# A fused attention and gated feed-forward kernel: weights converted in two VectorE passes, 42 tiles through the DMA crossbar instead of 28, and a new written order

## The chip, the cores and the metric

The kernel runs on one core of one Trainium2 chip. The metric is device time in microseconds (us) of that core, the median of several runs. A core has five engines with a queue each: TensorE (PE in the profile, PEld for its weight loads), VectorE (DVE), ScalarE (ACT), GpSimd (POOL) and SyncE (SP), which here only issues DMAs. A DMA's data is moved by 16 shared DMA engines. PE writes its results into PSUM, a small memory that VectorE and ScalarE can read.

## The reference

Eight batches, eight heads, 576 tokens, 64 columns per head, all fp32. Attention keeps only the scores within `tau` of a row's maximum; its output (512 columns) goes through a feed-forward layer with a gate that is a convolution over three tokens:

```python
scores = scale * np.matmul(q, k.transpose(0, 1, 3, 2))
thresh = np.max(scores, axis=-1, keepdims=True) - tau
scores = np.where(scores >= thresh, scores, -1000000000.0)
attn = np.exp(scores - np.max(scores, axis=-1, keepdims=True))
attn = attn / (np.sum(attn, axis=-1, keepdims=True) + 1e-09)
x = np.matmul(attn, v)                      # heads side by side: 512 columns
h = np.maximum(x @ w_in, 0.0)               # 1024 columns
conv = sum(conv_w[k] * hp[:, k:k + S] for k in range(3))   # hp: h, padded by one token
out = (h / (1.0 + np.exp(-conv))) @ w_out
```

The weights `w_in`, `w_out` and `conv_w` come as float64, which the chip has no arithmetic for: the kernel puts each together from its two 32-bit words.

## The kernel before, in words

**Pairs, tiles, chunks.** Heads go in pairs, four pairs to a batch. The 576 query rows of a batch are four tiles of 128 and one of 64; a batch is done in two chunks, tiles 0 and 1 and then tiles 2, 3 and 4. A *unit* is one tile of one pair; there are 160, counted in order (units 0 to 19 are the first batch). Odd pairs take the tiles of a chunk in reverse.

**A unit** (`unit`, L552). PE makes the scores of both heads into two PSUM tiles `ps_s` (L573 for the first batch, in plain fp32, and for 64-row tiles; L580 for the rest, with q in two parts). For each head VectorE takes the row maximum (L588), ScalarE the exponential (L597), one of three engines the limit "maximum minus tau" (L594, L592), and VectorE masks the exponentials by it and sums them (L600). Small steps make the inverse of the sum (L617, L624) and a shift for rows whose sum is zero (L621), and GpSimd normalises `em` (L633). There are two `ps_s` buffers, so the scores of the next unit wait for the masks of this one.

**Turning `em`.** The product with V needs `em` turned. For most tiles PE does it with 128x128 transposes (L692), and ScalarE takes them out of PSUM into `eT` (L687). Twenty-eight tiles, one for each even pair of each chunk from the second batch on (`CROSS`, L54 and L646), go through the DMA crossbar instead (`cross`, L648): ScalarE and GpSimd split `em` into its 16-bit halves (`parts`, L326 and L328), SP writes them to DRAM (`rows`, L665) and issues two crossbar transfers into `eT` (L670). PE then multiplies with V (L747, L756); from the third chunk on it does so for two pairs at a time, once both are turned.

**Feed-forward.** `mm1` (L772) multiplies by `w_in` (L784), with values and weights each in a high and a low part; then come ReLU (L799), two taps (L806), tanh (L813), gate (L811) and a split of the result (L821, L333). GpSimd sets the padding columns of `hp` each time (L794, L796). `mm2` (L833) multiplies by `w_out` (L842) and writes the output.

**Weights** (`split`, L353). Sixteen pieces of 128x512 are loaded during the first batch. For each: ScalarE takes the absolute value of the upper word (L377), GpSimd clamps it (L380), VectorE shifts it (L383), puts the sign in (L386) and adds bits of the lower word (L389); ScalarE rounds this to the high part (L400), and PE or GpSimd makes the low part (L405, L406, L333). The convolution weights need a row of some fifteen small VectorE steps more (`ratios`, L452 to L456).

**What sets the order.** Every step is recorded with a cost, a due time and its dependences (`Plan.op`, L101). `Plan.run` (L120) walks through them with assumed latencies (`LATENCY`, `late`) and writes each engine's instructions down in the order in which that walk picks them; ready steps go by due time less a lead (`AHEAD`), and PE stays with one kind of matmul for a while (`KEEP`). What it writes is fixed: on the chip every engine takes its queue strictly in this order and waits where an input is missing. The program spreads the feed-forward work of a chunk between the units of the next.

Of the kernel before, what the change touches and what calls it, by code (L numbers as in the profile page):

```python
# [19 lines left out]
TINY = 2.0 ** -15  # L20
HUGE = 3.0e38
AHEAD = {'s': 6.25, 's4': 7.75, 't': 3.5, 'a': 3.5, 'prep': 4.25, 'w': 2.5, 'load': 7.75}

LATENCY = {"pe": 210.0, "act": 145.0, "dve": 110.0, "pool": 75.0, "ring": 950.0}

HOLD = {"pool": 165.0, "dve": 130.0}

NORM = (('pool',), ('pool',))

NEAR = 8  # L30
# [5 lines left out]
WRATE = (1.225, 1.745)  # L36
ALT = 11.76
# [216 lines left out]
def tile_tau_attention_gated_ffn(  # L254
# [59 lines left out]
    ntau = const("ntau", [P, 1], F32)  # L314
    op("dve", 70, lambda: nc.vector.tensor_scalar(ntau[:], tau_sb[:], -1.0, None, op0=ALU.mult), w=[(ntau, 0)], r=[(tau_sb, 0)], ahead=6.0)
# [20 lines left out]
    def put(n, fn, issue=460, rows=P, queue="sp", **kw):  # L336


        op(queue, issue, fn, ring=rows * (n * 0.225 + 4) * 0.0737, **kw)
# [13 lines left out]
    def split(src, n, name, high, low, hr, lr, queue="sp"):  # L353
# [4 lines left out]
        value = plan.buf(wk, "q2", 2, [P, 2, 2 * P], U32, f"{name}_f")  # L358
# [17 lines left out]
        def f0():  # L376
            nc.scalar.activation(v(), words(F32)[1], AF.Abs)  # L377

        def f1(e):
            engines[e].tensor_scalar(v(), v(), HUGE, TINY, op0=ALU.min, op1=ALU.max)  # L380

        def f2():
            nc.vector.tensor_scalar(v(U32), v(U32), 3, 0x3FFFFFF8, op0=ALU.logical_shift_left, op1=ALU.bitwise_and)  # L383

        def f3():
            nc.vector.scalar_tensor_tensor(v(U32), words()[1], 0xC0000000, v(U32), op0=ALU.bitwise_and, op1=ALU.bitwise_or)  # L386

        def f4():
            nc.vector.scalar_tensor_tensor(v(U32), words()[0], 29, v(U32), op0=ALU.logical_shift_right, op1=ALU.bitwise_or)  # L389
# [40 lines left out]
    def load_conv():  # L430
# [25 lines left out]
        op("dve", 1100, ratios, w=[(cw, 0), (cr, 0)], r=[(cwl, 0)])  # L456
# [49 lines left out]
    def halves(dst, src, of, ahead):  # L506

        x, view, parts = src
        for part, head in of:
# [5 lines left out]
                ), issue=560, rows=D,  # L515
# [17 lines left out]
    def prep_q(i, b, p, q1, q2):  # L533
# [5 lines left out]
        op("act", act(w), lambda: nc.scalar.activation(q1[:, 0], xq[:], AF.Copy), w=[(q1, (0, 0)), (q1, (0, 1))], r=[(xq, 0)], ahead=a)  # L539
        op(  # L540
            "pool", pool(w), lambda e: subtract(e, q2[:, 0], xq[:], q1[:, 0].bitcast(F32)),
            w=[(q2, (0, 0)), (q2, (0, 1))], r=[(xq, 0), (q1, (0, 0)), (q1, (0, 1))], ahead=a, other=[("dve", dve(w))], port=True
        )
        for q in (q1, q2):
            halves(q, (q, Later(lambda q=q: q[:, 0], w), ((0, 0), (0, 1))), [((1, 1), 1), ((1, 0), 1), ((0, 1), 0)], a)

    def load_v(i, b, p):
        vt = plan.buf(wk, "v", 2, [P, NBLK, D], F32, f"v_{i}")
# [3 lines left out]
    def unit(u, k, q1, q2, o, n):  # L552
# [7 lines left out]
        few = plan.buf(sm, "few", 4, [P, 10], F32, f"few_{u}")  # L560
        a = AHEAD["s" if 2 * n > P else "s4"]
        tiny = [("pool", 200)]
        for h, js in enumerate(heads):
            ps = plan.buf(ps_s, "ps_s", 2, [P, 2, 512], F32, f"ps_s_{u}_{h}")
            nm, th, total = (slice(at + h, at + h + 1) for at in (0, 2, 4))

            def mm(h=h, js=js, ps=ps):
                if q2 is None:
                    for r, j in enumerate(js):
                        for c in range(2):  # L570
# [3 lines left out]
                                ps[r * n:(r + 1) * n, c, :CH], lhsT=q1[on, j, o:o + n], rhs=k[on, at:at + CH],  # L574
# [3 lines left out]
                for c in range(2):  # L578
                    for i, q in enumerate((q1, q2)):
                        nc.tensor.matmul(  # L580
                            ps[:, c, :CH], lhsT=q[:, h, o:o + n], rhs=k[:, h, c * CH:(c + 1) * CH], start=(i == 0), stop=(i == 1)
                        )
# [7 lines left out]
            def limit(e, nm=nm, th=th):  # L590
                if e == "act":
                    nc.scalar.activation(few[:rows, th], few[:rows, nm], AF.Identity, scale=-1.0, bias=ntau[:rows])  # L592
                else:
                    engines[e].tensor_scalar(few[:rows, th], few[:rows, nm], -1.0, ntau[:rows], op0=ALU.mult, op1=ALU.add)  # L594
# [4 lines left out]
            def mask(ps=ps, th=th, view=view, total=total):  # L599
# [411 lines left out]
```

## Time and profile before

| | |
|---|---|
| three runs | 912.18, 912.48, 914.12 us; median 912.48 us |
| span of the profiled execution | 910.8 us |
| mean granted TensorE clock in it | 0.993 |
| DMA traffic | 137.02 MB, mean 150 GB/s |
| SP's DMA issues | 336 copies `q<-q`, 64 loads of v, 28 writes of `rows`, 56 crossbar transfers |

The profile shows one execution; its own time is known as the span, from the first to the last instruction. The median of the runs lies 1.7 us above the span, so what lies around the span is about that. Each row of a group has the line of the kernel, the engine, the operation, what it writes and reads, and how often; then its busy time in us, the mean of one in ns, and the idle time of the engine just before it. Matmuls overlap, so what one of them takes from PE is read from one start to the next, not from its own length.

### The profile page before, as it was taken

How to read it: one execution, taken by the hardware profiler on the slowest of the kernel's cores; microseconds unless marked ns; L12 is line 12 of the kernel's file. 1: busy time of each engine (PE TensorE's matmuls, PEld its weight loads, DVE VectorE, ACT ScalarE, POOL GpSimd, SP SyncE). 2: the span in 40 equal slices, each digit the busy share in tenths (PEclk: the TensorE clock that was granted, in tenths of full speed). 3: DMA queues.
4: the chain of work that ended last, by engine and by line, in shares of the span. 5: the costliest groups of instructions: out<-in, count | busy, mean ns of one | idle time of the engine just before them, and what ended most of it. 6: DMA issues, size and time to landing. Idle time of an engine off the chain costs nothing.

```text
span 910.8 us, 19147 instructions
## 1 busy us (share of the span) xinstructions
PE 874.6 (96%) x6056; PEld 708.6 (78%) x6056; DVE 751.2 (82%) x1871; ACT 673.8 (74%) x1459; POOL 603.5 (66%) x1027
## 2 busy tenths in 40 slices
PE   5978799999999999999999999999999999999998
PEld 3545577878878788888788797887888878887896
DVE  5988999988988689987889789996988779997542
ACT  4878687878777777777768687877867778776642
POOL 2656778875767677685767767776776758675322
PEclk9989899999999999999999999999999999999999
DMA  6555257667764667647665377557667276654000
GB/s 213 155 162 170 57 143 197 149 178 181 198 175 113 163 175 198 158 116 202 169 157 157 117 201 191 140 118 202 173 176 179 89 187 159 181 137 112 13 24 35
DMA packets 148260, 137.02 MB, mean 150 GB/s; under 512 B 85312, under 2 KB 116288, under 8 KB 148160
## 3 DMA queue, kind: packets, MB, share of 16 engines
q1 hardware_dynamic: 147296, 133.90, 55.3%
q10 hardware_dynamic: 864, 1.90, 0.6%
q8 instruction: 49, 0.80, 0.4%
q14 instruction: 51, 0.42, 0.2%
HBM read 58.88 MB, written 25.95 MB: 93 GB/s over the span
## 4 chain that ended last, share of the span: by engine, by line
PE 73%; ACT 8%; DVE 6%; POOL 5%; DMA 4%; issue 3%; SPq 2%; ACTq 0%; POOLq 0%; DVEq 0%
PE po L842 20%; PE ph L784 16%; PE pa L756 12%; PE ps_s L580 11%; PE ps_t L692 9%; PE ps_s L573 3%; ACT em L597 2%; POOL em L633 2%; DVE em L600 2%; ACT eT L687 2%; PE pa L747 2%; DVE few L588 2%; DMA q<-in_qd_dram 1%; SPq L513 1%; DMA q<-q 1%
## 5 line engine op out<-in xcount | busy, mean ns | idle before, releaser
L633 POOL TENSOR_SCALAR em<-em,few 128x576 f32<-128x576 f32 x287 | 262.8, 924 | 29.9 <-DVE few L624 22.1
L600 DVE SCALAR_TENSOR_TENSOR em<-ps_s,few,em 128x576 f32<-128x576 f32 x288 | 230.5, 812 | 25.4 <-ACT em L597 17.1
L588 DVE TENSOR_REDUCE few<-ps_s 128x1 f32<-128x576 f32 x288 | 211.5, 748 | 39.3 <-PE ps_s L573 22.0
L597 ACT ACTIVATE em<-ps_s,few 128x576 f32<-128x576 f32 x288 | 210.5, 741 | 35.8 <-DVE few L588 31.5
L784 PE MATMUL ph<-x,w1h 128*128 128x322 f32 (+1 forms) x1024 | 233.7, 304 | 0.6 <-ACT hp L799 0.5
L687 ACT ACTIVATE eT<-ps_t 128x512 f32<-128x512 f32 (+2 forms) x360 | 168.0, 487 | 24.5 <-PE ps_t L692 22.4
L784 PEld LDWEIGHTS ph<-x,w1h 128*128 128x128 f32 x1024 | 173.1, 189 | 4.7 <-issue 3.0
L692 PE MATMUL ps_t<-ident,em 128*128 128x128 f32 x1060 | 157.8, 280 | 6.5 <-POOL em L633 5.1
L580 PE MATMUL ps_s<-ks,q 128*128 128x288 f32 x896 | 156.8, 306 | 5.3 <-DMA q<-q 2.1
L784 PE MATMUL ph<-x,w1l 128*128 128x322 f32 (+1 forms) x512 | 151.3, 295 | 0.0
L692 PEld LDWEIGHTS ps_t<-ident,em 128*128 128x128 f32 x1060 | 126.5, 143 | 31.5 <-POOL em L633 14.9
L580 PEld LDWEIGHTS ps_s<-ks,q 128*128 128x128 f32 x896 | 129.2, 189 | 20.2 <-issue 8.2
L333 POOL TENSOR_TENSOR gl<-t,gh 128x255 fp32r<-128x255 f32 (+9 forms) x192 | 119.6, 637 | 28.5 <-ACT gh L821 27.5
L756 PE MATMUL pa<-eT,v 128*64 128x320 f32 (+1 forms) x1024 | 132.1, 410 | 0.0
L842 PE MATMUL po<-w2h,gh 128*128 128x512 f32 x288 | 117.9, 409 | 0.3 <-ACT hp L799 0.3
L756 PEld LDWEIGHTS pa<-eT,v 128*64 128x64 f32 x1024 | 70.4, 137 | 59.3 <-issue 15.8
L842 PE MATMUL po<-w2l,gh 128*128 128x512 f32 x288 | 113.3, 393 | 0.0
L842 PE MATMUL po<-w2h,gl 128*128 128x512 f32 x288 | 113.1, 393 | 0.1
L806 DVE SCALAR_TENSOR_TENSOR t<-hp,cr 128x321 f32<-128x321 f32 (+1 forms) x128 | 75.6, 594 | 28.0 <-ACT hp L799 28.0
L784 PEld LDWEIGHTS ph<-x,w1l 128*128 128x128 f32 x512 | 96.8, 189 | 0.2
L813 ACT ACTIVATE t<-t,cm 128x321 f32<-128x321 f32 (+1 forms) x128 | 68.0, 535 | 25.2 <-DVE t L806 12.2
L811 DVE SCALAR_TENSOR_TENSOR t<-t,hp 128x321 f32<-128x321 f32 (+1 forms) x128 | 73.1, 573 | 11.4 <-ACT t L813 9.8
(80 smaller groups left out, 1104.1 us busy)
## 6 DMA issues: line engine op xcount, KB each, us to landing
q<-q SPq DMA_DIRECT2D x336, 64.0 KB, 2.1
v<-in_vc_dram SPq DMA_DIRECT2D x64, 288.0 KB, 3.8
rows<-parts SPq DMA_DIRECT2D x28, 576.0 KB, 3.3
k<-in_kp_dram SPq DMA_DIRECT2D x35, 320.0 KB, 3.5
out_dram<-ot SPq DMA_DIRECT2D x36, 256.0 KB, 2.3
xk<-in_kt_dram SPq DMA_DIRECT2D x28, 288.0 KB, 3.4
ks<-xk SPq DMA_DIRECT2D x56, 144.0 KB, 3.3
xq<-in_qt_dram SPq DMA_DIRECT2D x56, 128.0 KB, 2.9
```

Source lines behind the costliest of these rows:

```text
L333: engines[e].tensor_tensor(dst, x, y, op=ALU.subtract)
L580: nc.tensor.matmul(ps[:, c, :CH], lhsT=q[:, h, o:o + n], rhs=k[:, h, c * CH:(c + 1) * CH], start=(i == 0), stop=(i == 1))
L588: nc.vector.tensor_reduce(few[:rows, nm], ps[:rows, :, :CH], op=ALU.max, axis=mybir.AxisListType.XY, negate=True)
L597: nc.scalar.activation(view(), ps[:rows, :, :CH], AF.Exp, bias=few[:rows, nm])
L600: nc.vector.scalar_tensor_tensor(view(), ps[:rows, :, :CH], few[:rows, th], view(), op0=ALU.is_ge, op1=ALU.mult, accum_out=few[:rows, total])
L633: engines[e].tensor_scalar(sl, sl, by, to, op0=ALU.mult, op1=ALU.add)
L687: "act", act(w, True), lambda dst=dst, src=src: nc.scalar.activation(dst(), src(pt), AF.Copy),
L692: nc.tensor.transpose(out=pt[:, at:at + P], in_=em[:, int(b * P):int(b * P) + P], identity=ident[:])
L756: nc.tensor.matmul(pa[j * D:(j + 1) * D, :w], lhsT=vt[:, blk, :], rhs=eT[:, :w // D, blk, :], start=False, stop=(r == 3))
L784: nc.tensor.matmul(ph[:, :an], lhsT=w1[w][:, cb, fs], rhs=xs[cb][:, h, :an], start=(cb == 0 and i == 0), stop=(cb == NCB - 1 and i == 2))
L806: nc.vector.scalar_tensor_tensor(t[:, :kn], hp[:, k:kn + k], cr[:, j, f:f + 1], y, op0=ALU.mult, op1=ALU.add)
L842: nc.tensor.matmul(po[:], lhsT=x[:, f, at:at + P], rhs=w[:, f, :], start=(f == 0 and i == 0), stop=(f == NFB - 1 and i == 2))
```

## The change

The lines of the changed kernel are given as it has them; they are up to 28 further down.

- **Crossbar.** `CROSS` now depends on chunk and pair. In a batch's first chunk even pairs cross one tile as before; in its second chunk all four pairs do. There are 42 crossed tiles. `parts` has one buffer instead of two.
- **Weights.** ScalarE scales the absolute value by 2^-112, which takes the clamp's place, and a second ScalarE pass brings the lower word's top bits into place; VectorE shifts and puts the sign in; GpSimd adds the two.
- **Limits.** A unit's small values lie in four fixed tiles with `tau` written beside each maximum once. One VectorE reduction over the pair (maximum, tau) makes both heads' limits; it needs both maxima, and both masks come after it. In the same way one reduction adds a tiny constant to the sums, which replaces guard and shift.
- **Normalising.** From unit 16 on, one in four goes to ScalarE, with one more small VectorE step for its unit.
- **v and q.** A pair's v is loaded once per batch and kept (four buffers instead of two; the first batch still loads it twice). q's two parts lie in one tile, and each of the three copies moves both parts.
- **Padding.** `hp` has three fixed tiles whose padding columns are set once, at the start.
- **Order.** Leads, latencies, and costs of the walk have new values (the row of small steps counts as 2700 ns instead of 1100, for one), so every engine's order is new.

```diff
-AHEAD = {'s': 6.25, 's4': 7.75, 't': 3.5, 'a': 3.5, 'prep': 4.25, 'w': 2.5, 'load': 7.75}
+AHEAD = {'mask': -0.546, 'norm': 0.0, 'parts': 0.747, 'gate': 0.0, 'evac': 0.244, 'low': 0.0, 's': 8.8, 's4': 7.75, 't': 2.623, 'a': 4.072, 'prep': 5.282, 'w': 2.013, 'load': 10.996}
-NORM = (('pool',), ('pool',))
+NORM = (('pool',), ('pool', 'pool', 'pool', 'act'))
-CROSS = (1, 0)
+CROSS = ((1, 0, 1, 0), (1, 1, 1, 1))
...
         def f0():
-            nc.scalar.activation(v(), words(F32)[1], AF.Abs)
+            nc.scalar.activation(v(), words(F32)[1], AF.Abs, scale=2.0 ** -112)
-        def f1(e):
-            engines[e].tensor_scalar(v(), v(), HUGE, TINY, op0=ALU.min, op1=ALU.max)
+        def f1():
+            tops = flat().bitcast(U16).rearrange("p (f four) -> p f four", four=4)
+            nc.scalar.activation(words(I32)[0], tops[:, :, 1], AF.Copy, scale=2.0 ** -13)
         def f2():
-            nc.vector.tensor_scalar(v(U32), v(U32), 3, 0x3FFFFFF8, op0=ALU.logical_shift_left, op1=ALU.bitwise_and)
+            nc.vector.tensor_scalar(v(U32), v(U32), 3, None, op0=ALU.logical_shift_left)
         def f4():
-            nc.vector.scalar_tensor_tensor(v(U32), words()[0], 29, v(U32), op0=ALU.logical_shift_right, op1=ALU.bitwise_or)
+            nc.gpsimd.tensor_tensor(v(I32), v(I32), words(I32)[0], op=ALU.add)
...
-        op("dve", 1100, ratios, w=[(cw, 0), (cr, 0)], r=[(cwl, 0)])
+        op("dve", 2700, ratios, w=[(cw, 0), (cr, 0)], r=[(cwl, 0)])
...
-            def limit(e, nm=nm, th=th):
-                if e == "act":
-                    nc.scalar.activation(few[:rows, th], few[:rows, nm], AF.Identity, scale=-1.0, bias=ntau[:rows])
-                else:
-                    engines[e].tensor_scalar(few[:rows, th], few[:rows, nm], -1.0, ntau[:rows], op0=ALU.mult, op1=ALU.add)
+            def limit():
+                pairs = few[:rows, :2 * m].rearrange("p (h two) -> p h two", two=2)
+                nc.vector.tensor_reduce(few[:rows, 8:8 + m], pairs, negate=True, **add)
...
     def load_v(i, b, p):
-        vt = plan.buf(wk, "v", 2, [P, NBLK, D], F32, f"v_{i}")
+        if b and chunks[pairs[i][0]].new[0]:
+            return vts[i - NP]
+        vt = plan.buf(wk, "v", VB, [P, NBLK, D], F32, f"v_{i}")
...
-        return not plain(chunks[c].b) and t in [x for x in order(i) if TILES[x][1] == P][:CROSS[p % 2]]
+        return not plain(chunks[c].b) and t in [x for x in order(i) if TILES[x][1] == P][:CROSS[c % 2][p]]
```

Two places of the new order. On VectorE, in the first batch, the end of the row of small steps (`cm`, `cr`) before; `few_7` and `em_7` belong to unit 7, `stage_4` and `stage_5` are pieces of weights:

```order
L454 TENSOR_TENSOR cm_517<-cm_517 128x8 x2
L454 SCALAR_TENSOR_TENSOR cm_517<-cm_517,cw_491 128x8
L454 RECIPROCAL cm_517<-cm_517 128x8
L454 TENSOR_TENSOR cr_512<-cw_491,cm_517 128x8 x2
L588 TENSOR_REDUCE few_7_468<-ps_s_7_1_543 128x1
L383 TENSOR_SCALAR stage_4_f_541<-stage_4_f_541 128x512
L383 TENSOR_SCALAR stage_5_f_546<-stage_5_f_546 128x512
L386 SCALAR_TENSOR_TENSOR stage_4_f_541<-stage_4_336,stage_4_f_541 128x512
L600 SCALAR_TENSOR_TENSOR em_7_478,few_7_468<-ps_s_7_1_543,few_7_468,em_7_478 128x576
```

And now, where the row of small steps falls into unit 6:

```order
L467 TENSOR_TENSOR cm_440<-cm_440 128x8 x2
L467 SCALAR_TENSOR_TENSOR cm_440<-cm_440,cw_404 128x8
L467 RECIPROCAL cm_440<-cm_440 128x8
L467 TENSOR_TENSOR cr_435<-cw_404,cm_440 128x8 x2
L622 SCALAR_TENSOR_TENSOR em_6_422,few2_85<-ps_s_6_0_401,few2_85,em_6_422 128x576
L622 SCALAR_TENSOR_TENSOR em_6_422,few2_85<-ps_s_6_1_410,few2_85,em_6_422 128x576
L793 TENSOR_TENSOR x_1_465<-pa_1_417,x_1_465 128x256
L643 TENSOR_REDUCE few2_85<-few2_85 128x2
L612 TENSOR_REDUCE few3_87<-ps_s_7_0_473 128x1
```

The maximum and the passes over weights that stood between the small steps and the next mask have moved ahead of the small steps or behind the masks.

On SP, in the second chunk of a batch, from the write of a crossed tile (`rows_54`, unit 54) to its crossbar transfers, before; `xq`, `xk`, `ks` and `q` belong to later units:

```order
L665 DMA rows_54_3939<-parts_54_3915 128x2304
L538 DMA xq_26_3945<-in_qt_dram 128x256
L513 DMA q2_24_3910<-q2_24_3910 64x256
L850 DMA out_0_dram<-ot_7_3959 128x512
L523 DMA xk_3_0_3975<-in_kt_dram 128x576
L523 DMA xk_3_1_3984<-in_kt_dram 128x576
L493 DMA q_28_3992<-in_qd_dram 128x2x64
L493 DMA q_29_3994<-in_qd_dram 128x2x64
L513 DMA ks_3_0_4018<-ks_3_0_4018 64x576
L549 DMA v_22_4036<-in_vc_dram 128x576
L670 DMA_TRANSPOSE eT_22_4038<-rows_54_3939 128x9x128 x2
```

And now, at the next crossed tile of that chunk (unit 58, of an odd pair):

```order
L697 DMA_TRANSPOSE eT_22_3762<-rows_54_3609 128x9x128 x2
L692 DMA rows_58_3806<-parts_58_3770 128x2304
L526 DMA ks_3_0_3728<-xk_3_0_3653 64x576
L570 DMA v_24_3821<-in_vc_dram 128x576
L526 DMA ks_3_1_3743<-xk_3_1_3671 64x576 x2
L560 DMA qs_25_3804<-qs_25_3804 64x2x256 x2
L697 DMA_TRANSPOSE eT_23_3855<-rows_58_3806 128x9x128 x2
```

A second crossed tile follows right behind the transfers of the first, and fewer transfers stand between a write and its crossbar transfers.

More of the change, by code (lines that the diff above doesn't have):

```diff
@@ L13 @@
 I64 = mybir.dt.int64
+I32 = mybir.dt.int32
 U32 = mybir.dt.uint32
@@ L336, in put @@
     def put(n, fn, issue=460, rows=P, queue="sp", **kw):
-        op(queue, issue, fn, ring=rows * (n * 0.225 + 4) * 0.0737, **kw)
+        kw.setdefault("late", LATE["load"])
+        op(queue, issue, fn, ring=rows * n * 0.0149, **kw)
     def act(n, psum=False):
@@ L605, in unit @@
             op(
-                "pe", 490 if q2 is None else 534, mm, w=[(ps, 0)],
-                r=[(x, j) for x in (k, q1) for j in js] if q2 is None else [(x, (h, i)) for x in (k, q1, q2) for i in range(2)], ahead=a, kind="rows" if q2 is None else "full"
+                "pe", 534 if split else 490, mm, w=[(ps, 0)],
+                r=[(k, (h, i)) for i in range(2)] + [(q, (x, h, i)) for x in range(2) for i in range(2)] if split else [(x, j) for x in (k, q) for j in js], ahead=a, kind="full" if split else "rows"
@@ L613, in unit @@
-        ss = [(few, ("sum", h)) for h in range(m)]
-        sums, inverse, shift = slice(4, 4 + m), slice(6, 6 + m), slice(8, 8 + m)
-        def guard(e):
-            engines[e].tensor_scalar(few[:rows, inverse], few[:rows, sums], 1e-9, 1.0, op0=ALU.add, op1=ALU.mult)
-        def even(e):
-            engines[e].tensor_scalar(few[:rows, shift], few[:rows, sums], 0.0, 1.0 / S, op0=ALU.is_equal, op1=ALU.mult)
-        op("dve", 112, guard, w=[(few, "inverse")], r=ss, ahead=a, port=True, other=tiny)
@@ L624, in unit @@
-        op("dve", 82, lambda: nc.vector.reciprocal(few[:rows, inverse], few[:rows, inverse]), w=[(few, "inverse")], ahead=a)
-        op("dve", 124, even, w=[(few, "shift")], r=ss, ahead=a, port=True, other=tiny)
-        for h in range(m):
+            late.append(mask)
+            if h == m - 1:
+                op("dve", 85, limit, w=[(few, "th")], r=[(few, ("nm", x)) for x in range(m)], ahead=a)
+        for h in range(m):
+            op("dve", 738, late[h], w=[(em, h), (few, ("sum", h))], r=[(pss[h], 0), (few, "th")], ahead=a + AHEAD["mask"])
@@ new lines, in unit, with guard @@
+        ss = [(few, ("sum", h)) for h in range(m)]
+        inverse = slice(10, 10 + m)
+        def guard():
+            pairs = few[:rows, 4:4 + 2 * m].rearrange("p (h two) -> p h two", two=2)
+            nc.vector.tensor_reduce(few[:rows, inverse], pairs, **add)
+        op("dve", 85, guard, w=[(few, "inverse")], r=ss, ahead=a)
+        op("dve", 82, lambda: nc.vector.reciprocal(few[:rows, inverse], few[:rows, inverse]), w=[(few, "inverse")], ahead=a)
+        turns = NORM[u >= NEAR]
+        homes = [turns[(u * 2 + h) % len(turns)] for h in range(m)]
@@ L638, in unit @@
             op(
-                home, choice[home], norm, w=[(em, h)], r=[(few, "inverse"), (few, "shift")], ahead=a, port=True,
+                home, choice[home], norm, w=[(em, h)], r=[(few, "least" if "act" in homes else "inverse")], ahead=a + AHEAD["norm"], port=True,
                 other=[(e, ns) for e, ns in choice.items() if e != home]
```

151 lines of the change are left out of this document (84 added, 67 removed).

## The prediction

> **What bounds the kernel now.** I read the page's first part, then the table by stage, then the PE rows of the stages in which PE is not full, then the chain of waits inside a full stage. The page says who is busiest over the whole span:
>
> ```profile
> span 910.8 us, 19147 instructions
> PE 874.6 (96%) x6056; PEld 708.6 (78%) x6056; DVE 751.2 (82%) x1871; ACT 673.8 (74%) x1459; POOL 603.5 (66%) x1027
> ```
>
> The table by stage (time in us; then busy time of PE, PEld, DVE, ACT and POOL; granted clock; DMA share; GB/s) shows that this mean covers two different stages:
>
> ```profile
> 47.00:52.00 5.00, 0.50 (x6) 0.05 (x2) 4.76 (x17) 1.89 (x4) 1.51 (x3) 0.91 0.57 196
> 52.00:58.00 6.00, 5.86 (x16) 3.64 (x17) 4.32 (x10) 4.16 (x8) 3.19 (x5) 0.51 0.57 174
> 101.00:108.00 7.00, 2.07 (x23) 1.13 (x21) 7.00 (x15) 3.80 (x7) 3.83 (x5) 0.84 0.22 61
> 108.00:113.00 5.00, 4.99 (x26) 3.04 (x19) 4.33 (x15) 4.25 (x9) 4.71 (x6) 0.55 0.44 110
> 150.00:500.00 350.00, 345.96 (x2506) 290.22 (x2506) 303.35 (x776) 268.50 (x585) 248.70 (x416) 1.00 0.65 166
> 500.00:850.00 350.00, 347.37 (x2473) 289.62 (x2472) 294.94 (x742) 266.47 (x578) 244.29 (x424) 1.00 0.59 155
> ```
>
> From 150 to 850 us PE works 693.3 of 700 us, and no other engine passes 87%. There a microsecond of PE work taken away is a microsecond of span, as long as nothing else comes late. Before that lies the first batch, with the conversion of the weights beside it. It has two holes, at 47 to 52 and at 101 to 108, and behind each hole PE runs at about half its clock. The PE rows (start, length, instruction; in brackets the idle time before it and what ended it):
>
> ```profile
> 46.26 1.24 PE L573 MATMUL ps_s<-k,q 64*128 64x288 f32 x8
> 52.14 0.85 PE L573 MATMUL ps_s<-k,q 64*128 64x288 f32 x2 [4.63 <-DVE em L600]
> 101.48 0.28 PE L784 MATMUL ph<-x,w1h 128*128 128x256 f32 x1
> 103.75 0.72 PE L573 MATMUL ps_s<-k,q 64*64 64x288 f32 x8 [2.00 <-DVE em L600]
> 107.40 2.50 PE L573 MATMUL ps_s<-k,q 64*64 64x288 f32 x12 [2.93 <-issue]
> ```
>
> Together these holes are 4.63 + 2.00 + 2.93 = 9.6 us. The half clock behind them costs 6.00 x (1 - 0.51) + 5.00 x (1 - 0.55) = 5.2 us more. So 14.8 us of the start hang on two waits for VectorE's masks.
>
> **The change part by part.** *Fourteen more tiles through the crossbar.* An uncrossed full tile of two heads has nine 128x128 transposes on PE; 28 crossed tiles become 42, so 14 x 9 = 126 transposes go (1060 to 934 in the order). The price is what one takes from its start to the next start. The chain of waits in the full stage gives it, and the slots of the other PE instructions too:
>
> ```profile
> 179.43 2.10 PE po L842 x9
> 235.30 2.12 PE ph L784 x18
> 237.42 0.44 PE ps_t L692 x4
> 237.86 0.53 PE ps_s L580 x4
> ```
>
> A transpose is 0.44 / 4 = 0.110 us, so 126 x 0.110 = 13.9 us leave PE, all behind 110 us. Its order on PE also changes kind of matmul less often (489 times for 524); that can only take a little off, and I cost it at nothing.
>
> What takes their place runs elsewhere: per tile a split on ScalarE and one on GpSimd, one write to DRAM, and two crossbar transfers that SP issues. The groups:
>
> ```profile
> L328 POOL COPY parts<-em 128x1152 uint16<-128x1152 uint16 x28 | 33.7, 1204 | 0.7
> L326 ACT ACTIVATE parts<-em 128x1152 uint16<-128x1152 uint16 x28 | 32.6, 1165 | 1.3 <-POOL em L633 0.8
> rows<-parts SPq DMA_DIRECT2D x28, 576.0 KB, 3.3
> eT<-rows SPq DMA_TRANSPOSE x56, 4.3
> ```
>
> These are 14 x 1.204 = 17 us on GpSimd and 14 x 1.165 = 16 us on ScalarE, off the path by their shares above. The latency is another matter: PE must not reach the product with V (L774 in the new kernel) before the transfer has landed, and if it does, everything queued on PE stands behind it. One crossed tile of before, scores to product:
>
> ```profile
> 216.92 1.31 PE L580 MATMUL ps_s<-ks,q 128*128 128x288 f32 x8
> 228.04 0.54 SPq L665 DMA_DIRECT2D rows<-parts  x1
> 231.95 4.05 SPq L670 DMA_TRANSPOSE eT<-rows  x2
> 252.24 0.66 PE L747 MATMUL pa<-eT,v 64*64 64x256 f32 x8
> ```
>
> The scores end at 218.2. The second transfer is issued at about 234 and lands some 4.3 us later, at 238.3: a chain of 20.1 us, with 14 us to spare. In the new order PE's cover is shorter for the tiles of odd pairs, which are new. The last of them (unit 158) has 24 L863, 69 L812, 28 transposes and 8 score matmuls between its scores and its product. By the slots above (2.10 / 9, 2.12 / 18, 0.110, 0.53 / 4) that is 5.6 + 8.1 + 3.1 + 1.1 = 17.9 us, 2.2 us short of the chain. Worked in the same way, the 14 odd-pair tiles have 17.5 to 24.6 us, and six of them under 20.1, together some 6.6 us short. Against that, the new SP order has six transfers between a write and its crossbar transfers where nine stood (at the two places shown with the change), so the chain should get shorter. I take 2.5 us of new PE waits, between 0 (the chain shrinks with its queue) and 6.6, and more in a rival.
>
> *Weights.* Of three VectorE passes and one GpSimd pass on each of 16 pieces, one VectorE pass (L389) goes; ScalarE gets one more pass and GpSimd an add of two tensors for the cheaper clamp.
>
> ```profile
> L389 DVE SCALAR_TENSOR_TENSOR stage_f<-stage,stage_f 128x512 uint32<-128x512 uint32 x16 | 13.8, 864 | 0.0
> L380 POOL TENSOR_SCALAR stage_f<-stage_f 128x512 f32<-128x512 f32 x16 | 10.5, 658 | 8.0 <-ACT stage_f L377 7.6
> L333 POOL TENSOR_TENSOR w2l<-stage_f,w2h 128x512 fp32r<-128x512 f32 x4 | 5.7, 1433 | 3.2 <-ACT w2h L400 3.2
> ```
>
> VectorE loses 13.8 us, all in the start stage. GpSimd swaps 10.5 us for at most 16 x 1.433 = 22.9: the integer add isn't in the trace, its bounds are the one-input pass at 0.658 and this two-input one, and I take the upper since it has two inputs. ScalarE's extra pass lies between nothing gained and the 0.867 of a 576-wide pass (below), so at most 14 us.
>
> *Limits, sums and normalising.* The 288 limits were spread over three engines; 160 pair sums on VectorE replace them. Guard and shift become one pair sum; 57 normalisings move from GpSimd to ScalarE, each unit of these with one more small VectorE step.
>
> ```profile
> L594 DVE TENSOR_SCALAR few<-few,ntau 128x1 f32<-128x1 f32 x170 | 33.1, 208 | 1.0
> L617 DVE TENSOR_SCALAR few<-few 128x2 f32<-128x2 f32 (+1 forms) x69 | 20.2, 293 | 1.0
> L621 DVE TENSOR_SCALAR few<-few 128x2 f32<-128x2 f32 (+1 forms) x93 | 14.9, 160 | 0.0
> L624 DVE RECIPROCAL few<-few 128x2 f32<-128x2 f32 (+1 forms) x160 | 25.5, 160 | 1.4 <-POOL few L617 0.2
> L633 POOL TENSOR_SCALAR em<-em,few 128x576 f32<-128x576 f32 x287 | 262.8, 924 | 29.9 <-DVE few L624 22.1 <-DVE few L594 6.1 <-DMA ks<-xk 0.3
> L631 ACT ACTIVATE em<-em,few 128x576 f32<-128x576 f32 x1 | 0.9, 867 | 0.0
> ```
>
> A reduction over a pair isn't in the trace; its bounds are 0.160 and 0.293 of other two-column steps, and I take 0.160, the row of the step that shares no port (L624). VectorE then changes by 377 x 0.160 - 33.1 - 20.2 - 14.9 = -8 us (+42 at 0.293). With the weights it ends near 729 us of 751, at worst 779, under PE either way. ScalarE gains at most 57 x 0.867 + 16 + 14 = 80 us, to 754 before its 28 saved evacuations are taken off: 85% of the new span, so it isn't the bound. GpSimd loses 56 x 0.924 = 52 us. The new wait, mask of head 0 for the maximum of head 1, has little to hold: in 118 of the 128 two-head units VectorE already had both maxima ahead of the first mask. Behind the mask stand the next unit's maxima, and PE waits for them only if its queue holds no feed-forward work.
>
> *v kept, q's copies joined.* Twenty-eight loads of v and half of q's 336 copies leave SP's queue; no PE wait above is theirs. I cost both at nothing: PE's other work hides them, and without it a load is worth about its landing, a few us once per batch.
>
> *The order of the start.* The first hole is VectorE's row of small steps on the convolution weights, then a maximum, passes over weights, and only then the mask that PE waits for:
>
> ```profile
> 45.86 0.18 DVE L454 TENSOR_TENSOR cw<-cw,cwl 128x24 f32<-128x24 f32 x1 [0.81 <-POOL cwl L333]
> 49.07 0.24 DVE L454 TENSOR_TENSOR cr<-cw,cm 128x8 f32<-128x8 f32 x2
> 49.23 0.75 DVE L588 TENSOR_REDUCE few<-ps_s 128x1 f32<-128x576 f32 x1
> 49.90 0.76 DVE L383 TENSOR_SCALAR stage_f<-stage_f 128x512 uint32<-128x512 uint32 x2
> 51.17 0.81 DVE L600 SCALAR_TENSOR_TENSOR em<-ps_s,few,em 128x576 f32<-128x576 f32 x1
> ```
>
> The small steps take 3.4 us and stay. In the new order the mask stands right behind them, so 51.17 - 49.31 = 1.9 us of the 4.63 go and 2.8 stay. At the second hole, VectorE is at 7.00 of 7 us; the new order has the last four pieces of weights there with two passes each, and both masks of a unit together, with PE's feed-forward matmuls between the scores. I let that hole (4.9 us) and the half clock behind it (2.2) go. That is 1.9 + 4.9 + 2.2 = 9.0; I give back 1.0 for waits that the new order makes at other places and take 8 (from 0 to 14.8).
>
> The Trainium skill, in TensorE: Matmul & The Clock Gate (HAM oscillation), warns of PE idle gaps over about 3.4 us, after which the clock is halved. The trace agrees behind 4.63 us (clock 0.51) and behind 2.00 and 2.93 with little between them (0.55). By that rule a first hole of 2.8 us keeps the full clock, and the sum would be 2.9 us lower than mine.
>
> The sum against the profiled execution: 910.8 - 13.9 - 8.0 + 2.5 = 891.4 us of span. The median of the runs shown, 912.48, lies 1.7 above that span, so the forecast is 891.4 + 1.7 = **893.1 us**.
>
> **The rivals.**
>
> *The start is cleared, the crossbar hides* (0.15): both holes and both half clocks go and no product waits: 910.8 - 13.9 - 14.8 + 1.7 = 883.8. For it speaks VectorE's relief by a third of its weight passes; against it that the 3.4 us of small steps stay.
>
> *The start's waits only move* (0.20): as much is lost at new places, since ScalarE now also carries a second weight pass, and GpSimd a longer one, in the stage that has the least cover: 910.8 - 13.9 + 2.5 + 1.7 = 901.1.
>
> *The crossbar comes late, slower* (0.08): the write, two transfers and their queue take so long that each added tile holds PE. From 21.9 / 14 = 1.6 us for each the kernel is slower than before; at 2 us it is 14 x 2 = 28, and 910.8 - 13.9 - 8.0 + 28 + 1.7 = 918.6. For it: covers of 17.5 to 20 us against a chain of 20.1. Against it: by the chain shown no cover is more than 2.6 us short, and eight of the 14 not at all.
>
> *A transpose frees its whole duration* (0.02): one has a mean of 280 ns in its group,
>
> ```profile
> L692 PE MATMUL ps_t<-ident,em 128*128 128x128 f32 x1060 | 157.8, 280 | 6.5 <-POOL em L633 5.1 <-ACT eT L687 0.8 <-POOL xk L333 0.4
> ```
>
> and 126 x 0.280 = 35.3 would make 910.8 - 35.3 - 8.0 + 2.5 + 1.7 = 871.7. But 1060 x 0.280 is 297 us where the group is busy for 157.8, so they overlap. The Trainium skill, on the same page (Part 4: PE-mode transpose), gives about 275 ns for one in a kernel; by that figure 126 are an estimated 35 us. The row has the same duration, and the 0.110 between starts decides against it.
>
> *Nothing moves* (0.05): the freed slots are filled by waits for VectorE, which stays at 84% or so: 912.5.
>
> **How the numbers follow.** The forecast itself (a start that gains 4 to 10 us, crossbar waits of 0 to 7) has 0.50, from 889 to 900. The range goes from 881, under the cleared start, to 908, over the moved waits with the unknown prices on top; it leaves out the late crossbar, no change, and the whole duration, 0.15. Under 0.2% (1.8 us) a measurement of this kernel can't tell from no change. Faster: 0.50 + 0.15 + 0.20 + 0.02 = 0.87; same 0.05; slower 0.08.
>
> **What would show it.** Right: 934 transposes; PE busy near 860 us; between 150 and 850 still 98% or more; the hole at the small steps under 3.5 us and no half clock at 101 to 113; PE waits for eT transfers of a few us in all. Wrong: PE rows at the product with V that wait for the crossbar by more than 1.6 us each; a stage of the full part with PE under 95%; ScalarE over 90%; new holes of several us in the first 150 us with a half clock behind them.

## The result, and the profile after

The changed kernel takes 890.0 us (median of four runs, 888.02 to 891.74) against 913.13 for the kernel before (four runs, 912.18 to 914.12): a ratio of 0.974, with a 95% interval of 0.972 to 0.976. The forecast was 893.1. One run of a kernel further down (v in two buffers) took 1209.93 us at a granted clock of 0.66 where all others have 0.99 or more, and is left out of that kernel's median. The profiled execution is the slowest of the four, with a span of 889.9 us, 20.9 less than before; so the trace accounts for 20.9 of the 23.1 us between the medians. Its page begins:

```profile
span 889.9 us, 18227 instructions
PE 861.2 (97%) x5930; PEld 691.7 (78%) x5930; DVE 748.0 (84%) x1902; ACT 712.5 (80%) x1489; POOL 476.8 (54%) x617
```

The stages of the prediction (us; busy PE, PEld, DVE, ACT, POOL; clock; DMA share; GB/s), in the changed kernel:

```profile
47.00:52.00 5.00, 4.42 (x26) 2.65 (x25) 4.88 (x13) 4.30 (x10) 3.93 (x4) 0.92 0.54 168
52.00:58.00 6.00, 6.00 (x37) 3.34 (x37) 5.38 (x14) 5.01 (x10) 3.99 (x6) 1.00 0.61 196
101.00:108.00 7.00, 6.57 (x51) 5.38 (x52) 6.69 (x16) 6.36 (x14) 6.29 (x7) 1.00 0.49 125
108.00:113.00 5.00, 5.00 (x36) 2.62 (x35) 4.20 (x11) 4.23 (x11) 2.95 (x4) 1.00 0.67 195
150.00:500.00 350.00, 348.41 (x2454) 287.84 (x2453) 310.25 (x806) 292.88 (x609) 196.97 (x258) 1.00 0.69 178
500.00:850.00 350.00, 347.11 (x2473) 286.38 (x2472) 294.47 (x755) 279.42 (x593) 185.77 (x244) 1.00 0.63 163
```

The second hole is gone: PE has 11.57 of 12 us at 101 to 113, where it had 7.06, and the clock stays at 1.00. The start of ScalarE's and PE's queues, before and then in the changed kernel, and what is left of the first hole (start, length; in brackets the idle time before and what ended it):

```profile
3.90 2.04 ACTq L374 DMA_DIRECT2D stage<-in_w_in_dram  x3
...
6.45 2.46 PE L573 MATMUL ps_s<-k,q 64*128 64x288 f32 x8 [6.45 <-ACT q L503]
```

```profile
3.65 4.57 ACTq L386 DMA_DIRECT2D stage<-in_w_in_dram  x3
...
8.27 0.72 ACT L516 ACTIVATE qs<-qs 128x256 f32<-128x256 f32 x2 [5.12 <-DMA k<-in_kp_dram]
...
8.73 2.29 PE L597 MATMUL ps_s<-k,qs 64*128 64x288 f32 x8 [8.73 <-ACT qs L516]
...
44.31 2.25 PE L597 MATMUL ps_s<-k,qs 64*128 64x288 f32 x8 [2.15 <-DVE em L622]
```

So the first hole fell from 4.63 to 2.15 us, but PE begins 2.3 us later than before (8.73 for 6.45). The issues of three weight loads on ScalarE's queue now take 4.57 us instead of 2.04: by the trace the third is issued at 7.89, when a load of k lands (7.87) whose semaphore this weight load uses in turn. The scalings of q, and with them the first matmul, stand behind it on the queue.

A ledger by two stretches for each kernel, before and then after (the first column behind the length is PE's busy time):

```profile
0.00:150.00 150.00, 124.30 (x740) 79.74 (x741) 126.99 (x308) 112.62 (x231) 93.98 (x152) 0.95 0.52 156
150.00:910.80 760.80, 750.33 (x5318) 628.91 (x5317) 624.24 (x1565) 561.16 (x1228) 509.55 (x876) 1.00 0.57 149
```

```profile
0.00:150.00 150.00, 129.45 (x816) 85.31 (x817) 128.94 (x318) 126.18 (x259) 86.15 (x109) 0.99 0.55 164
150.00:889.90 739.90, 731.79 (x5116) 606.39 (x5114) 619.08 (x1585) 586.32 (x1231) 390.66 (x509) 1.00 0.63 163
```

PE's idle time in the first 150 us goes from 25.7 to 20.55 (-5.2), behind it from 10.5 to 8.1 (-2.4), and its busy time falls by 13.4; together that is the 20.9. Part of the busy time is the clock. Before, PE worked 10.92 us in two stretches at half clock (first row, their sum); now it works 3.41 us in one:

```profile
sum 13.66, PE 10.92 PEld 6.76 DVE 11.38 ACT 9.29 POOL 9.23; mean PE 5.46 PEld 3.38 DVE 5.69 ACT 4.64 POOL 4.62
```

```profile
44.40:47.81 3.41, 3.41 (x14) 2.42 (x15) 2.94 (x8) 0.90 (x2) 1.42 (x3) 0.50 0.09 14
```

At full clock this work would take half the time, so half of the difference, 3.75 us, is work done faster. That makes an estimate by stage: the start gives 5.2 + 3.75 = 8.9 us (8.0 forecast), and the full stage 13.4 - 3.75 = 9.7 of work and 2.4 of waits, 12.1 us (13.9 - 2.5 = 11.4 forecast). No PE wait in the full stage is for a crossbar transfer; the largest from 150 to 850 us (us in total, times, longest):

```profile
PE ps_t L719 <- ACT eT L714: 1.3, 5, 0.3
PE ph L812 <- ACT hp L821: 0.5, 1, 0.5
```

Groups that answer to those the prediction priced:

```profile
L719 PE MATMUL ps_t<-ident,em 128*128 128x128 f32 x934 | 137.0, 277 | 5.1 <-ACT eT L714 3.3 <-POOL em L660 0.8 <-DVE few L616 0.3
...
L616 DVE TENSOR_REDUCE few<-few 128x2 f32<-128x4 f32 (+1 forms) x160 | 23.9, 150 | 1.8
...
L651 DVE TENSOR_SCALAR few<-few 128x2 f32<-128x2 f32 x57 | 16.5, 290 | 0.6
...
L827 DVE SCALAR_TENSOR_TENSOR t<-hp,cr 128x321 f32<-128x321 f32 (+1 forms) x128 | 82.4, 645 | 22.7 <-ACT hp L821 21.3 <-ACT t L834 0.8 <-POOL gl L344 0.4
```

### The profile page after: what moved, and what is told of

It is laid out like the page before. It is cut to its first block, busy times and chain, and to the rows that moved or that the text cites. A ratio compares the mean times of both kernels' runs of the same rounds, so it can differ in the third digit from the quotient of the medians.

```text
span 889.9 us, 18227 instructions
## 1 busy us (share of the span) xinstructions
PE 861.2 (97%) x5930; PEld 691.7 (78%) x5930; DVE 748.0 (84%) x1902; ACT 712.5 (80%) x1489; POOL 476.8 (54%) x617
## 4 chain that ended last, share of the span: by engine, by line
PE 80%; ACT 9%; DVE 6%; DMA 3%; issue 2%; SPq 0%; POOL 0%; ACTq 0%; DVEq 0%
PE po L863 20%; PE ph L812 19%; PE ps_s L604 13%; PE pa L783 12%; PE ps_t L719 9%; PE ps_s L597 4%; DVE em L622 2%; ACT eT L714 2%; ACT em L619 2%; PE pa L774 2%; DVE few L612 2%; DMA xk<-in_kt_dram 1%; PE pw_stage L418 1%; DMA k<-in_kp_dram 1%; DMA ks<-xk 1%
## 5 line engine op out<-in xcount | busy, mean ns | idle before, releaser
L660 POOL TENSOR_SCALAR em<-em,few 128x576 f32<-128x576 f32 x231 | 190.7, 832 | 185.9 <-DVE few L646 151.3
L812 PE MATMUL ph<-x,w1h 128*128 128x322 f32 (+1 forms) x1024 | 238.4, 304 | 0.5 <-ACT hp L821 0.5
L622 DVE SCALAR_TENSOR_TENSOR em<-ps_s,few,em 128x576 f32<-128x576 f32 x288 | 225.3, 811 | 14.6 <-ACT em L619 8.5
L714 ACT ACTIVATE eT<-ps_t 128x512 f32<-128x512 f32 (+2 forms) x332 | 149.1, 474 | 10.6 <-PE ps_t L719 8.4
L604 PE MATMUL ps_s<-ks,qs 128*128 128x288 f32 x896 | 151.9, 304 | 2.6 <-DVE em L622 0.6
L604 PEld LDWEIGHTS ps_s<-ks,qs 128*128 128x128 f32 x896 | 127.5, 188 | 27.5 <-issue 19.7
L719 PE MATMUL ps_t<-ident,em 128*128 128x128 f32 x934 | 137.0, 277 | 5.1 <-ACT eT L714 3.3
L719 PEld LDWEIGHTS ps_t<-ident,em 128*128 128x128 f32 x934 | 109.1, 142 | 27.5 <-issue 8.0
L827 DVE SCALAR_TENSOR_TENSOR t<-hp,cr 128x321 f32<-128x321 f32 (+1 forms) x128 | 82.4, 645 | 22.7 <-ACT hp L821 21.3
L832 DVE SCALAR_TENSOR_TENSOR t<-t,hp 128x321 f32<-128x321 f32 (+1 forms) x128 | 76.7, 600 | 12.6 <-ACT t L834 12.0
L827 DVE SCALAR_TENSOR_TENSOR t<-hp,cr,t 128x321 f32<-128x321 f32 (+1 forms) x128 | 85.7, 672 | 0.5
```

Source lines behind the costliest of these rows:

```text
L604: nc.tensor.matmul(ps[:, c, :CH], lhsT=q[:, i, h, o:o + n], rhs=k[:, h, c * CH:(c + 1) * CH], start=(i == 0), stop=(i == 1))
L622: nc.vector.scalar_tensor_tensor(view(), ps[:rows, :, :CH], few[:rows, th], view(), op0=ALU.is_ge, op1=ALU.mult, accum_out=few[:rows, total])
L660: engines[e].tensor_scalar(sl, sl, LEAST, few[:rows, 10 + h:11 + h], op0=ALU.add, op1=ALU.mult)
L714: "act", act(w, True), lambda dst=dst, src=src: nc.scalar.activation(dst(), src(pt), AF.Copy),
L719: nc.tensor.transpose(out=pt[:, at:at + P], in_=em[:, int(b * P):int(b * P) + P], identity=ident[:])
L812: nc.tensor.matmul(ph[:, :an], lhsT=w1[w][:, cb, fs], rhs=xs[cb][:, h, :an], start=(cb == 0 and i == 0), stop=(cb == NCB - 1 and i == 2))
```

## The experiments

The forecast came out, so the question was whether for its reasons: that the full stage's gain is 126 transposes less on a full PE, and that the order matters only in the start. Kernels that keep the planner make a new order with every edit. Others have the order of the changed kernel written out instruction by instruction, so that one thing changes and nothing moves. Ratios are to the kernel before, measured on the same chip. The groups of runs come from several chips, on which the kernel before has medians from 913.13 to 915.05 us; a difference in us between kernels of two groups is therefore sure only to some 2 us.

**The tiles, out of the new kernel and into the old one.**

```diff
 # the new kernel
-CROSS = ((1, 0, 1, 0), (1, 1, 1, 1))
+CROSS = ((1, 0, 1, 0), (1, 0, 1, 0))
```

> The new kernel with 28 crossbar tiles instead of 42; all else stays. Theory (a transpose costs PE the 0.110 us between two starts, and the added crossbar tiles hide): the 126 transposes come back for 126 x 0.110 = 13.9 us, all in the full stage, so 890.0 + 13.9 = 903.9 us, with the start as in the new kernel (unit 20's scores at about 118 us). Rival 1 (a transpose costs its whole 0.28 us): 890.0 + 35 = 925. Rival 2 (the full stage's gain comes from the rest of the change, not from the tiles): 890 to 893.

Measured: 910.69 us, ratio 0.995 (0.994 to 0.997). The tiles carry 20.7 us (19.4 by the two ratios), more than their 13.9 and far from 35. In its ledger PE's busy time (877.2 us) is 16.0 above the new kernel's and its idle time 3.1 (start 20.1, later 11.7); in the full stage PE waits longest for VectorE's masks, 5.4 us where the new kernel has 0.2:

```profile
150.00:909.00 759.00, 747.29 (x5244) 620.52 (x5242) 620.04 (x1585) 587.54 (x1245) 376.88 (x495) 1.00 0.53 137
```

```profile
PE ps_s L604 <- DVE em L622: 5.4, 9, 0.9
```

```diff
 # the kernel before
-CROSS = (1, 0)
+CROSS = ((1, 0, 1, 0), (1, 1, 1, 1))
-[:CROSS[p % 2]]
+[:CROSS[c % 2][p]]
```

> The kernel before with 42 crossbar tiles by the new table; all else stays, with its own priorities and SP order. Theory (the tiles alone carry the full stage's gain, and the crossbar hides without the new priorities): 913.1 - 13.9 = 899.2 us, no PE wait for a crossbar transfer. Rival 1 (the new priorities of SP's transfers are what keeps the transfers ahead of the product): PE waits at the product with V for eT on the added tiles, some 2 us each, and the time lies at 900 to 920. Rival 2 (nothing): 913.

Measured: 914.23 us, ratio 0.999 (0.997 to 1.001). The theory falls: the same 126 transposes are gone from PE (934 are left), and the time has not moved. The stretch behind 150 us and the sum of both, and then the longest of PE's waits in the full stage (us in total, times, longest):

```profile
150.00:913.10 763.10, 745.57 (x5203) 614.73 (x5200) 651.98 (x1559) 562.35 (x1220) 528.55 (x899) 1.00 0.65 171
sum 913.10, PE 867.92 PEld 692.32 DVE 778.03 ACT 673.93 POOL 621.50; mean PE 433.96 PEld 346.16 DVE 389.01 ACT 336.96 POOL 310.75
```

```profile
PE ph L784 <- ACT ot L849: 2.0, 2, 1.1
PE pa L747 <- DMA q<-q: 1.9, 1, 1.9
PE ps_t L692 <- ACT eT L687: 1.5, 2, 1.0
```

PE's busy time fell by only 6.7 us (why by so little is open), and its idle time behind 150 us rose from 10.5 to 17.5, mostly in short waits for ScalarE and VectorE. Rival 1's mechanism is there, but once: at the product with V PE waits 1.9 us. The view puts this wait down to a copy of q, which the product does not read. By the landing times in the trace no copy of q came in while PE waited, from 757.01 to 758.92 us: those issued from 756.11 on landed from 759.3 on. The second of the crossbar transfers ahead of them on SP landed at 758.67:

```profile
751.56 3.81 SPq L670 DMA_TRANSPOSE eT<-rows  x2
...
758.92 0.76 PE L747 MATMUL pa<-eT,v 64*64 64x320 f32 x4 [1.91 <-DMA q<-q]
```

So a crossbar transfer came late by 1.9 us; the rest of the 7.0 us of new idle time is in other waits.

**The order.** The new kernel with the planner's tables of before (the costs of single steps and the assumed time of a transfer stay new):

```diff
-AHEAD = {..., 's': 8.8, 't': 2.623, 'a': 4.072, 'prep': 5.282, 'w': 2.013, 'load': 10.996}
+AHEAD = {..., 's': 6.25, 't': 3.5, 'a': 3.5, 'prep': 4.25, 'w': 2.5, 'load': 7.75}
 # and LATENCY, HOLD, WRATE, ALT, KEEP of before; LATE = 0, 0, -500, 100
```

> The new kernel with the planner's numbers of before (AHEAD, LATENCY, HOLD, WRATE, ALT, LATE, KEEP); the operations stay the new ones. Theory (the numbers carry the start's gain and the absence of crossbar waits, the operations the rest): 890.0 plus about 5 of the start plus 0 to 7 of crossbar waits, 895 to 902 us. Rival 1 (the numbers are worth nothing; the operations carry all): 888 to 892. Rival 2 (the whole gain is the order's): 909 or more.

Measured: 912.53 us, ratio 0.997 (0.994 to 1.000). Rival 2: without the new numbers next to nothing is left of the gain (0.3%), although the operations are the new ones. PE's idle time behind 150 us is 24.0 us. The stretch, and the waits of the full stage:

```profile
150.00:910.40 760.40, 736.41 (x5154) 610.34 (x5150) 631.49 (x1593) 589.00 (x1240) 395.88 (x516) 1.00 0.61 159
```

```profile
PE ph L812 <- ACT hp L821: 5.9, 5, 2.6
PE ps_t L719 <- DVE x L793: 4.3, 4, 1.2
PE ps_t L719 <- ACT eT L714: 3.8, 4, 1.7
PE ps_s L604 <- DVE em L622: 3.4, 6, 1.0
```

The other way round, the kernel before with 42 tiles and the new numbers (`AHEAD`, `LATENCY`, `HOLD`, `WRATE`, `ALT`, `KEEP`, `LATE`, the new transfer time), its operations left alone:

> The kernel before with 42 crossbar tiles and the new planner's numbers where its operations have a place for them (due times, assumed latencies and transfer times, kind rules); operations of masks, weights, v and q as before. Theory A (the 42 tiles pay only in an order with more lead, and the numbers give it): 897 to 903 us, since the full stage gets its 14 and the start's gain stays out. Theory B (the numbers pay only with the new operations, which free VectorE and GpSimd): 908 to 916, PE waits for VectorE and GpSimd as in the kernel before with 42 tiles. Theory C (numbers and tiles are all of it): 890 to 893.

Measured: 924.21 us, ratio 1.011 (1.010 to 1.013), 1.1% slower than before. Theory B, and worse than it said. The start alone has 31.0 us of idle PE, and over the whole span PE now also waits for copies of q and k:

```profile
0.00:150.00 150.00, 119.04 (x716) 74.67 (x717) 126.08 (x312) 109.77 (x224) 91.21 (x147) 0.98 0.53 156
```

```profile
PE ps_s L575 <- DVE em L602: 11.5, 9, 3.5
...
PE ps_s L582 <- DMA ks<-xk: 4.1, 3, 1.7
...
PE ps_s L582 <- DMA q<-q: 3.7, 4, 2.7
```

Which of the numbers? First all due times of before (`AHEAD` as in the diff above), the rest new:

> The new kernel with the due times of before alone (scores 6.25 units ahead instead of 8.8, loads 7.75 instead of 11, and so on); assumed latencies, transfer times and kind rules stay the new ones. Theory (the lead of the scores is what lets PE run past short waits in the full stage): 903 to 913 us, as with all old numbers. Rival (the assumed latencies and transfer times carry it): 889 to 896.

Measured: 903.47 us, ratio 0.988 (0.986 to 0.989), 13.5 us above the new kernel, as the theory had it. Then a single one:

```diff
-'s': 8.8
+'s': 6.25
```

> The new kernel with one due time of before: the scores of two-head units 6.25 units ahead instead of 8.8; every other number stays new. Theory (the scores' lead is what the full stage lives on): most of the 13.5 us that all old due times cost come back, 898 to 904 us. Rival (no single due time carries it; they fit each other): 889 to 895.

Measured: 901.56 us, ratio 0.985 (0.983 to 0.987): 11.6 of the 13.5. This number is how many units before its turn a two-head unit's scores come due. With the old one PE is idle 2.0 us more in the start (22.5) and 5.5 more behind it (13.6), and busy 2.3 more. The largest part of it that has a name is the wait for the masks of VectorE that free the score buffers: 3.3 us in the full stage for 0.2, once long enough to lose half the clock. The rest is spread over small waits. The waits of the full stage, and two windows around the longest:

```profile
PE ps_s L604 <- DVE em L622: 3.3, 5, 1.9
PE ps_t L719 <- ACT eT L714: 1.9, 5, 0.6
```

```profile
218.30:221.70 3.40, 1.51 (x12) 1.28 (x11) 3.40 (x9) 3.34 (x8) 3.31 (x4) 1.00 0.71 139
221.70:225.10 3.40, 3.36 (x15) 2.88 (x14) 3.40 (x9) 2.83 (x7) 3.22 (x4) 0.50 0.97 233
```

Whether the good order is a lucky one, a neighbour tells:

```diff
-LATENCY = {'pe': 159.52, ...
+LATENCY = {'pe': 165.0, ...
```

> The new kernel with one number of the planner moved by 3% (the latency that it assumes behind PE, 165 for 159.52); same operations, another order. Theory (the order that these numbers give is a fitted one, and a neighbour of it loses part of the gain): 893 to 905 us, with more short PE waits in the full stage. Rival (the numbers carry the gain as a policy, and neighbours do as well): 888 to 892.

Measured: 890.05 us, ratio 0.973 (0.971 to 0.975). The rival: from some 115 rows (GpSimd) to 780 (PE) of an engine stand elsewhere, and the time is the same. It is one neighbour, by one number.

**A transpose in a fixed order.** The order written out, and 32 groups of four issued twice:

```diff
-lambda: parts(pt)
+lambda: [parts(pt) for _ in range(1 + twice(u, i))]   # both groups of four in 16 units
```

> The new kernel with its order kept, and 128 more 128x128 transposes in the full stage: 32 groups of four are issued twice in a row, the second time into the same place. Theory (a transpose costs PE the 0.110 us between two starts): 128 x 0.110 = 14.1 us more, 904.1 us. Rival 1 (the whole 0.277): 35 us more, 925. Rival 2 (PE's stage has slack that takes them up): under 5 us more. If it is 14, then of the 20.7 us that 28 tiles instead of 42 cost, the rest of 7 is order.

Measured: 899.60 us, ratio 0.984 (0.982 to 0.986), 9.6 us above the new kernel (and 9.6 and 10.3 above the kernels at 890.05 and 889.29, of the same group of runs). The 0.109 between two starts holds here too (a run of 16 transposes is 1.665 us long, one of 8 is 0.792), so 14 us were put on PE; but its busy time rose by 10.4, and its idle time behind 150 us fell from 8.1 to 5.7:

```profile
150.00:897.70 747.70, 741.96 (x5242) 620.25 (x5240) 617.93 (x1585) 587.78 (x1230) 390.50 (x509) 1.00 0.64 161
sum 897.70, PE 871.59 PEld 705.63 DVE 747.25 ACT 714.26 POOL 477.03; mean PE 435.79 PEld 352.82 DVE 373.63 ACT 357.13 POOL 238.51
```

So even this stage has some slack between its instructions. A transpose is worth about 9.6 / 128 = 0.075 us there, and 126 are 9.5 us. The rest of the 20.7 that the tiles are worth with a new order is what the order makes of them, or comes with the 28 passes of ScalarE out of PSUM that a crossed tile also saves; no run separates these two.

**v.** First v loaded twice for each batch into two buffers, as before, with a new order:

> The new kernel with v loaded twice for each batch into two buffers, as before. Theory (keeping v hides nothing that PE waits for, and the third early load of v is what delays the weight loads on ACT's queue and with them the first matmul by 2.3 us): first matmul at 6.4 us instead of 8.7, and 888 us. Rival 1 (28 more loads on SP's queue delay the crossbar): PE waits for eT, 892 or more. Rival 2 (nothing: first matmul still at 8.7): 890 within 1.5.

Measured: 902.01 us (three runs, 900.73 to 903.05), ratio 0.985 (0.981 to 0.989): 12.0 us lost. That is in the range of rival 1, but not by its cause, since PE never waits for a crossbar transfer (below). The first matmul did not come earlier (first row below). One more run gives a trace:

> The new kernel with v loaded twice for each batch into two buffers, once more, for its trace. Theory (a load of v now waits on SP's queue until the buffer's last product is done, and the crossbar's transfers stand behind it): about 902 us, PE waits for eT transfers or for q's copies in the full stage. Rival (the planner gives another order in which VectorE or ScalarE come late): 902 us, the PE waits of the full stage are for VectorE and ScalarE, and none for a transfer.

Measured: 903.52 us in one run. Over the whole span PE's waits are mostly the rival's, for ScalarE and VectorE. But the largest of the full stage, 2.4 us, is for a copy of q, which the theory named, so neither has it whole:

```profile
PE ps_s L595 <- ACT qs L516: 8.4, 1, 8.4
PE ps_t L717 <- ACT eT L712: 6.5, 10, 1.4
...
PE ps_s L602 <- DMA qs<-qs: 2.4, 2, 1.7
```

Then the 28 loads alone, with nothing moved: each behind the load of q's columns of its pair, into DRAM scratch.

```diff
+plan.extra[mark].append(lambda: nc.sync.dma_start(again[:], vc[b, p]))
```

> The new kernel with its order kept, and 28 more loads of v (the ones that the change took out), each issued on SP's queue behind the load of q's columns of the same pair, into DRAM scratch that nothing reads. Theory (kept v is worth nothing by itself; the 12 us of loading v twice with a new order are the order's): 890 within 1. Rival (the loads take SP's queue and DMA from the crossbar's transfers): 893 to 902, with PE waits for transfers.

Measured: 889.29 us, ratio 0.973 (0.971 to 0.975). The loads are worth nothing. So the 12.0 us come with the two buffers: from the order that the planner makes with them, or from waits for a free buffer, which no run separates.

**The first matmul.** On ScalarE's queue, order written out:

```diff
 DMA stage_1<-in_w_in
+ACTIVATE qs_0<-qs_0 x2
 DMA stage_2<-in_w_in
-ACTIVATE qs_0<-qs_0 x2
```

> The new kernel with its order of instructions written out and kept, and one change: on ScalarE's queue the third load of weights is issued behind the two scalings of q instead of ahead of them. Theory (in the new kernel this load waits on its queue until 7.9 us, and holds the two scalings and with them the first matmul, which starts at 8.7 us where it started at 6.4 before): the first matmul starts at about 6.3 us, and the time is 890.0 - 2.3 = 887.7 us. Rival (the start's other waits take it back, the masks of VectorE above all): the first matmul is earlier, and the time stays within 0.7 us of 890.

Measured: 888.07 us (887.25 to 888.32), ratio 0.971 (0.969 to 0.973), the fastest kernel here. It is 1.9 us under the new kernel, whose own runs spread by 3.7; but all five of its runs lie under all eight of the two kernels at 890.05 and 889.29 that were measured beside it. The trace shows the cause removed:

```profile
3.60 2.21 ACTq L266 DMA_DIRECT2D stage<-in_w_in_dram  x2
...
6.33 2.68 PE L477 MATMUL ps_s<-k,qs 64*128 64x288 f32 x8 [6.33 <-ACT qs L396]
```

So here a load that waits on an engine's queue held the arithmetic behind it. The theory of the test with two v buffers, that without an early third load of v the first matmul comes earlier, is not borne out: there a load of q took that place on SP's queue, and the wait stayed.

## Why the prediction was right, and where not

**The number** is right, 893.1 against 890.0, and by the ledger nearly so in both stages. Part of that is luck, since several errors offset each other: in the full stage a transpose was priced too high and waits were booked that did not come, and in the start gains and losses that nobody had priced took each other back.

**Transposes.** 934 are left, as said. The price of 0.110 between two starts is confirmed; what is wrong is to call it span. In a fixed order a transpose was worth about 0.075 (9.6 us for 128), so this term was some 9.5 us and not 13.9. The whole duration (the rival at 871.7) is out: 128 of them would have cost 35 us.

**"There a microsecond of PE work taken away is a microsecond of span, as long as nothing else comes late."** This is the step that failed as a rule. PE at 98% did not make it true: 126 transposes less were worth 0 in the kernel before, and 20.7 with the new planner's numbers and operations. The second half of the sentence carried everything, and the prediction looked only at the crossbar for what could come late. With the old numbers the other waits come late (17.5 and 24.0 us of idle PE behind 150 us, for 8.1 in the new kernel). So the rival "nothing moves", at 0.05, was what two of the experiments did. The forecast had its gain because the change brought new numbers as well, of which the lead of the scores alone is worth 11.6 us. The prediction took the order as an affair of the start and of SP's queue.

**Crossbar waits**, forecast as 2.5 us between 0 and 6.6: there were none. For the one tile that the prediction worked out, unit 158, the cover was right and the chain too long (PE's rows and SP's):

```profile
816.41 1.34 PE L604 MATMUL ps_s<-ks,qs 128*128 128x288 f32 x8
...
827.65 2.80 SPq L697 DMA_TRANSPOSE eT<-rows  x2
...
836.15 0.77 PE L774 MATMUL pa<-eT,v 64*64 64x320 f32 x8
```

From the scores' end to the product are 836.15 - 817.75 = 18.4 us (17.9 forecast). The transfers are issued from 827.65 on, the second at 829.0, and land a median of 4.0 us after their issue, at about 833: a chain of some 15 us, not 20.1. It shrank, as the lower bound had it.

**The start**, 8 us: about 8.9, in other shares. The first hole gave 2.5 (1.9 forecast), the second 4.5 of its 4.9; half clock gave 3.75 (2.2 forecast), although the first hole still leaves 3.41 us of it. PE's waits for normalised `em` fell from 5.1 to 0.8 us, which the prediction did not see. Against that stand the first matmul's 2.3 us, which it did not see either, and the waits for masks outside the holes: 5.6 us in nine, where they were 2.4 in two (the 1.0 that it gave back was for such waits).

**v kept and q's copies joined, at nothing.** For v's loads this is shown in a fixed order. The edit still has a consequence: with two buffers of v the kernel is 12.0 us slower. For q's copies nothing was tried alone; in the old operations with the new numbers PE waits 3.7 us for them.

**The other engines.** VectorE is at 748.0, not 729. The pair reductions are right (0.150 for 0.160). The small step L651 takes 0.290, 57 x 0.13 = 7.4 us more: 0.168 in the six cases with GpSimd at work over less than half of it, 0.304 in the others, where the pair reductions have 0.150 either way. Taps and gates, whose arithmetic stayed, grew by 15 us (85.7 + 82.4 + 76.7 for 81.0 + 75.6 + 73.1). In the full stage PE waits 0.6 us in all for VectorE, so there this cost little. ScalarE at 712.5 is under its 754, GpSimd's integer add at 1.338 us between its bounds.

**Open.** Which of the new operations the new numbers need (with the old operations they are slower than before), and why two buffers of v instead of four cost 12.0 us.

## What to carry to other kernels

Here a full engine's freed time became span only where its queue had ready work to put there. So take the work out in a kernel whose order stays, and ask of each other engine, not only of the new transfer, whether it keeps up. When a change brings new work and a new order together, neither can be priced from its own rows; undo each alone, and hold the order fixed where a number is wanted. In a kernel ordered by due times, look first at how far ahead the first step of a unit is due.

## What the runs showed of the hardware

**In these traces the clock follows PE's busy share of whole windows.** In the changed kernel a hole of 2.15 us was followed by half clock. The window ahead of the half-clock row 44.40:47.81 above:

```profile
41.00:44.40 3.40, 1.25 (x12) 0.66 (x9) 3.06 (x17) 2.76 (x7) 0.00 (x0) 1.00 0.31 92
```

PE was busy for 37% of this window, and ran the next at half. In the kernel with the shorter lead it was 44% (1.51 of 3.40), with a hole of 1.89. The traces of all thirteen kernels can be cut into such windows, starting from the clock's own changes. Of the windows at full clock before the kernel's end, 24 had PE busy under half, and 22 of them were followed by half clock; of those above half, one was (0.57). This count says nothing of windows already at half clock: in the kernel before, one with PE busy for 2.37 of 3.41 us was followed by another at half. The Trainium skill (TensorE: Matmul & The Clock Gate, Part 1) has a free-running window of about 3.4 us; the trace agrees with that, its stretches of half clock are 3.41 and 6.83 us. The Trainium skill's warning of idle gaps over 3.4 us (TensorE: Matmul & The Clock Gate, HAM oscillation) is too mild for this kernel.

**VectorE's taps and gates slow down beside GpSimd.** In the changed kernel one takes 0.49 us in the mean when GpSimd is at work over less than half of it (171 of them) and 0.76 when over more (213); where the split into `parts` alone covers more than half, 0.95 (twelve). When the kernel before got 14 more splits on GpSimd, these steps took 17.8 of the 26.8 us by which VectorE grew. The Trainium skill (Trainium Architecture — The Big Picture, What this means for kernel authors) names an exclusive port shared by just these two. The durations fit that, but no run here isolates the port.
